# A fourth seven-product pair of gate/value tiles in the middle blocks of a fused attention and GEGLU kernel

## The chip, the cores and the metric

The kernel runs on one core of one Trainium2 chip. A core has TensorE (matmuls, written PE in the profile, with PEld for its weight loads), VectorE (DVE), ScalarE (ACT), GpSimd (POOL) and SyncE (SP, which here only issues DMAs). Each engine works through its own queue of instructions in order, and the queues are tied together by semaphores. The metric is device time in microseconds (us), as a median of several runs; one more execution was profiled.

## The reference

There are eight batches (B = 8) of eight heads, 576 rows and 64 columns per head. For each head, q is put through a softmax over its 64 columns and k through a softmax over its 576 rows; the head's output is softmax(q) @ (softmax(k)^T @ v). The heads stand side by side as x, with 4608 rows and 512 columns. Then comes a gated feed-forward layer:

```
g   = x @ w_gate          # 512 x 1536
val = x @ w_val           # 512 x 1536
out = (gelu(g) * val) @ w_out      # 1536 x 512, gelu in the erf form
```

Inputs and output are float32. The kernel works in float16 with float32 accumulation.

## The kernel before

**Blocks.** Rows are worked in blocks. Each batch gives a block of 512 rows (blocks 0 to 7), and the 64 rows left over of each batch are gathered in `xtr` and make block 8. The order is 0 to 6, then 8, then 7 (`order`). A block has two stages. The first makes `ht` = gelu(x w_gate) * (x w_val), transposed, in twelve tiles of 128 hidden columns (`NFI` = 12, `NO` = 6). The second multiplies `ht` by w_out.

**Plain tiles.** A plain tile needs four 512-column matmuls with w_gate ("6g" in a list of steps) and four with w_val ("6v"); `half` issues one such half. ScalarE applies gelu to the gate half, and VectorE multiplies both into `ht` (`scalar_tensor_tensor`, L624).

**Pairs.** Two tiles k and k + 3 can be made together with Strassen's seven products instead of eight (`pair_step`, `product_gv` at L605). Each product is four 256-column matmuls, so that a pair takes 28 of them, and it needs sums of blocks of the weights (`ws`, made by `sum_wgv`, L586) and of x (`xs`, made by `sum_x` on GpSimd, L592). A pair has four steps, k.1 to k.4:

- k.1: product 1 into bank pa, which ScalarE copies to pb (L660), and product 5 into pc, which is copied scaled to SBUF as `snq` ("snap", L640 on ScalarE, L638 on VectorE)
- k.2: product 6 added to pa, then snapped, and product 3 added to pc; VectorE adds pc and the snap into `cc` (L644)
- k.3: product 7 added to pa, VectorE adds pa and the first snap into `cc`; product 2 added to pb. pb gives the left half of tile k (`final`: gelu of 256 columns on ScalarE, L630, then a multiply on VectorE, L631). `upper` then does gelu on `cc` (L648) and GpSimd multiplies (L650), which gives the right halves of both tiles
- k.4: product 4 added to pa, which gives the left half of tile k + 3

All eight PSUM banks form one ring from block 2 on (`big`, `let_go`); a pair holds three of them until its results are read.

**The order within a block.** It is written out by hand. `THREE` is the list of steps of blocks 2 to 6: tiles 6 to 11 but for those in pairs 0, 1 and 2 are plain (pair 0 is tiles 0 and 3, and so on), and they alternate with the steps of the three pairs. `SIX`, for blocks 8 and 7, makes all twelve tiles in six pairs, two at a time. Letters in these lists are hooks: `ride(b, PR, letter)` issues what `at(b, PR, letter, ...)` has put there. In blocks 2 to 6, "a" and "n" are the two halves of the softmax of the next batch's q (`norm_pair`: a reduce at L240 and a reciprocal at L242 on VectorE, then two multiplies on GpSimd, L249), "t" is the DMA that transposes it (`unit_td`), "l" loads for the batch after that, and "s0", "u0", "s1", "u1" are sums of `ht` for the output (`sum_h`, L575; sums 1 and 2 on VectorE, 3 and 4 on GpSimd).

**The output.** `out_strassen` also uses seven products, of twelve matmuls each (`product`, L712), with sums of `ht` (`sh`, `s4`) and of w_out (`tw`, made by `sum_w`, L556). Hooks `ride(b, NS, i)` stand between products: at 0 the products of k and v for the next batch (`unit_kv4`), at 2 the casts of v and sums of weights, at 4 the next x (`unit_x4`), whose VectorE share is the casts at L192, and its sums. "e" holds the exps of q and k. The left-over rows of batch 0 have a norm and a transpose of their own (`norm_rem0`, `unit_trem`).

**The weight sums before.** Those for pairs 0 to 2 are spread over blocks 0 and 1 in full width (three tiles, 128 x 768). Those for pairs 6 to 8, which blocks 8 and 7 use, are made one or two per block in blocks 2 to 6. Sum 3 overwrites a quarter of the weights in place (`a21`), so the plain tile that needs it must be done.

Of the kernel before, what the change touches and what calls it, by code (L numbers as in the profile page):

```python
# [18 lines left out]
def kernel(  # L19
# [10 lines left out]
    nc = tc.nc  # L30

    B, H, S, D = q.shape
# [202 lines left out]
    def norm_pair(b, g, n0, engs):  # L235

        n = NC - n0
        e = buf(eq_b, b)[:, n0:NC, 2 * g * P:(2 * g + 2) * P].rearrange("p n (h d) -> p n h d", d=D)
        rq = att.tile([P, n, 4], f32, name="rq2", tag="rq2", bufs=2)
        nc.vector.reduce_sum(rq, e, axis=mybir.AxisListType.X)  # L240
        rrq = att.tile([P, n, 4], f32, name="rrq2", tag="rrq2", bufs=2)
        nc.vector.reciprocal(out=rrq, in_=rq)  # L242
        for j, eng in enumerate(engs):
            st[(b, "norm", 2 * g + j)] = (e[:, :, 2 * j:2 * j + 2], rrq[:, :, 2 * j:2 * j + 2], n)
            norm_mul(b, 2 * g + j, eng)

    def norm_mul(b, hp, eng="dve"):
# [328 lines left out]

    def sum_wgv(nm, i, k=0, n=NO // 2, eng="dve"):
        w = wg_sb if nm == "g" else wv_sb  # L580
        lo, hi = slice(k * P, (k + n) * P), slice((k + NO // 2) * P, (k + NO // 2 + n) * P)
        a11, a21, a12, a22 = w[:, 0:2, lo], w[:, 0:2, hi], w[:, 2:4, lo], w[:, 2:4, hi]
        t = [ws[(nm, k // NO)][:, j, :, k % NO * P:(k % NO + n) * P] for j in range(3)]
        o, a, b, op = {1: (t[0], a21, a22, ALU.add), 2: (t[1], t[0], a11, ALU.subtract),
                       3: (a21, a11, a21, ALU.subtract), 4: (t[2], a12, t[1], ALU.subtract)}[i]
        (nc.gpsimd if eng == "pool" else nc.vector).tensor_tensor(out=o, in0=a, in1=b, op=op)  # L586

    def sum_x(xt, xs=xs):
        b11, b12, b21, b22 = (xt[:, c:c + 2, r:r + 256] for c in (0, 2) for r in (0, 256))
# [4 lines left out]
    def product_gv(i, ps, xt, k, first):  # L594
# [3 lines left out]
        for t, w, nm in ((0, wv_sb, "v"), (1, wg_sb, "g")):  # L598
            ss = ws[(nm, k // NO)]
            for c in range(2):  # L600
# [6 lines left out]

    THREE = ("a 6g l 6v 0.1 9g 0.2 9v 0.3 7g 0.4 n 1.1 t 7v 1.2 10g 1.3 s0 10v 1.4 2.1 u0 8g 2.2 s1"  # L610
             " 8v 2.3 u1 11g 2.4 11v")
    SIX = ("0.1 6.1 0.2 6.2 0.3 6.3 0.4 1.1 6.4 7.1 s0 1.2 7.2 1.3 u0 7.3 1.4 2.1 7.4 8.1 s1 2.2"
           " 8.2 2.3 u1 8.3 2.4")
    steps = {b: (SIX if b >= B - 1 else THREE).split() for b in range(2, B + 1)}
    live = {}

    def half(b, xt, c, nm):
# [9 lines left out]
    def pair_step(b, xt, k, i):  # L627
        def final(ps, fi):
            gl = ffn.tile([P, 256], f32, name="glq", tag="gl")
            nc.scalar.activation(out=gl, in_=ps[:, 1], func=ACTF.Gelu)  # L630
            nc.vector.scalar_tensor_tensor(out=ht[:, fi, 0:256], in0=ps[:, 0], scalar=_H_SCALE,  # L631
                                           in1=gl, op0=ALU.mult, op1=ALU.mult)
            let_go(ps)

        def snap(ps, dve=False):
            sn = ffn.tile([P, 2, 256], f32, name="snq", tag="snq")
            if dve:
                nc.vector.tensor_scalar(out=sn, in0=ps, scalar1=_H_SCALE, scalar2=None, op0=ALU.mult)  # L638
            else:
                nc.scalar.activation(out=sn, in_=ps, func=ACTF.Copy, scale=_H_SCALE)  # L640
            return sn

        def add(o, ps, sn):
            nc.vector.scalar_tensor_tensor(out=o, in0=ps, scalar=_H_SCALE, in1=sn,  # L644
                                           op0=ALU.mult, op1=ALU.add)

        def upper(cc):
            nc.scalar.activation(out=cc[:, :, 1], in_=cc[:, :, 1], func=ACTF.Gelu,  # L648
                                 scale=1.0 / _H_SCALE)
            (nc.vector if k == NFI - NO // 2 - 1 else nc.gpsimd).tensor_tensor(  # L650
                out=ht[:, k:k + NO // 2 + 1:NO // 2, 256:512], in0=cc[:, :, 0], in1=cc[:, :, 1],
                op=ALU.mult)

        if i == 1:
            live["odd"] = odd = b > 2 and not live.get("odd", True)
            cc = cc_b if odd else ffn.tile([P, 2, 2, 256], f32, name="cc", tag="cc", bufs=1)
            pa = big([P, 2, 256], f32, "pga", True)
            product_gv(1, pa, xt, k, True)
            pb = big([P, 2, 256], f32, "pgb", True, True)
            nc.scalar.copy(out=pb, in_=pa)  # L660
            pc = big([P, 2, 256], f32, "pgc", True)
            product_gv(5, pc, xt, k, True)
            live[k] = [cc, pa, pb, pc, snap(pc, b >= B - 1)]
            return
        cc, pa, pb, pc, s5 = live[k]
        if i == 2:
            product_gv(6, pa, xt, k, False)
            s2 = snap(pa)
            product_gv(3, pc, xt, k, False)
            add(cc[:, 0], pc, s2)  # L670
            let_go(pc)
        elif i == 3:
            product_gv(7, pa, xt, k, False)
            add(cc[:, 1], pa, s5)
            product_gv(2, pb, xt, k, False)
            final(pb, k)
            if k == NFI - NO // 2 - 1:
                live["upper"] = lambda: upper(cc)
            else:
                upper(cc)  # L680
        else:
            product_gv(4, pa, xt, k, False)
            final(pa, k + NO // 2)
# [18 lines left out]
    def product(i, ps, first, ts=(0, 1), js=range(NO)):  # L702
        for j in js:
            for t in ts:
                c0, c1 = slice(t * P, (t + 1) * P), slice(256 + t * P, 256 + (t + 1) * P)
                a = {1: ht[:, j, c0], 2: ht[:, NO + j, c0], 3: s4[:, j, c0], 4: ht[:, NO + j, c1],
                     5: sh[1][:, j, c0], 6: sh[2][:, j, c0], 7: ht[:, j, c1]}[i]
                w = {1: wo_sb[:, j, 0:256], 2: wo_sb[:, NO + j, 0:256],
                     3: wo_sb[:, NO + j, 256:512]}.get(i)
                if w is None:  # L710
                    w = tw[{4: 4, 5: 1, 6: 2, 7: 3}[i]][:, j]
                nc.tensor.matmul(ps[t], a, w, start=(first and j == js[0] and (  # L712
                    t == ts[0] or ps[t].tensor is not ps[ts[0]].tensor)),
                                 stop=(j == js[-1]), skip_group_check=True)
# [7 lines left out]
    def out_strassen(b, last):  # L722
# [30 lines left out]

        js = (0, 1, 2, 3, 4, 5) if b < 2 else (0, 3, 1, 4, 2, 5)
        get("a")
        product(1, ps["a"], True, js=js[:4])
        ride(b, NS, 0)
        if b >= B - 1:
            pair_step(b, get_x(b), NFI - NO // 2 - 1, 4)
# [15 lines left out]
        product(6, ps["a"], False, js=js)  # L775
        s2 = snap("a")
        ride(b, NS, 2)
        cut = NO - 1 if b < B - 2 else NO
        product(3, ps["c"], False, js=js[:cut])
        if cut < NO:  # L780
            product(7, ps["a"], False, js=js)
# [125 lines left out]
    def load_2nd():  # L907
# [6 lines left out]
    at(0, NS, 5, L(unit_t, 1, 0))  # L914
    at(0, NS, 16, L(unit_kv, 1, 0), L(cast_v, 1, 4, 8), L(load_batch, 2, ((v, "v"),)),
       L(norm, 1, 3))
    at(0, NS, 17, L(unit_x, 1, 0, "act", True), L(unit_x, 1, 1, "act", True), L(sum_w, 1, "pool"),
       L(sum_w, 3, "pool"))
    at(0, NS, 7, L(exp, "q", 2))
    first1 = [[L(unit_t, 1, 1), L(unit_kv, 1, 1)],  # L920
              [L(unit_x, 1, 2, "dve"), L(preload, ACTF.Gelu)],
# [8 lines left out]

    at(1, FI, 2, L(unit_trem, 1))
    at(1, FI, 3, L(norm, 2, 2, "pool"), L(load_batch, 3, ((q, "q"), (k, "k"))))
    at(1, FI, 4, L(exp, "k", 2, 0, 4), L(norm, 2, 3, "pool"), L(sum_w, 2), L(sum_w, 4), make_s)
    at(1, FI, 5, L(cast_v, 2, 0, H))
    at(1, FI, 8, L(unit_td, 2))
    at(1, FI, 11, L(exp, "k", 2, 4, 8), L(exp, "q", 3))
# [3 lines left out]
    load_2 = lambda n: load_batch(n, ((v, "v"), (q, "q"), (k, "k")))  # L940
    for i, x in enumerate(("g1", "v1", "g2", "v2", "g4", "v4")):
        at(0, FI, 5 + i, L(sum_wgv, x[0], int(x[1])))
    at(1, FI, NFI - 1, L(sum_wgv, "g", 3, 0, NO // 2, "pool"), L(sum_wgv, "v", 3, 0, NO // 2, "pool"))
    for b in range(2, B):
        n = b + 1
        if n < B:
            at(b, PR, "a", L(norm_pair, n, 0, 0, ("pool", "pool")))
            at(b, PR, "n", L(norm_pair, n, 1, 0, ("pool", "pool")))
            at(b, PR, "t", L(unit_td, n))
        if n + 1 < B:  # L950
            at(b, PR, "l", L(load_2, n + 1))
            at(b, NS, 2, L(cast_v, n + 1, 0, H))
            at(b, PR, "e", L(exp, "q", n + 1), L(exp, "k", n + 1))
    at(4, PR, "l", load_rem0)
    at(4, PR, "e", exp_rem0)
    at(6, PR, "t", L(unit_trem, 0))
    for b in range(2, B - 1):
        n = b + 1
        at(b, NS, 4, L(unit_x4, n, ("act", "dve"), 0 if n == B - 1 else None))
        at(b, NS, 0, L(unit_kv4, n, True))  # L960
        if b < 6:
            at(b, NS, 4, L(preload, ACTF.Gelu))
        at(b, NS, 4, L(lambda n: sum_x(get_x(n)), n if n < B - 1 else B))
        if b == 5:
            at(b, NS, 4, norm_rem0)
    at(B, NS, 2, L(lambda: sum_x(get_x(B - 1), xs_b[1])))
    for b in range(2, B + 1):
        for j in range(NO // 2 - 1):
            at(b, PR, f"s{j}", L(sum_h, j, NO, (1,)), L(sum_h, j, NO, (3,), "pool"))
            at(b, PR, f"u{j}", L(sum_h, j, NO, (2,)), L(sum_h, j, NO, (4,), "pool"))  # L970
    for b, x in ((2, "g1"), (2, "g2"), (3, "v1"), (3, "v2"), (4, "g4"), (5, "v4"), (6, "g3"), (6, "v3")):
        at(b, NS, 2, L(sum_wgv, x[0], int(x[1]), NO, NO // 2))


    def ride(b, kind, i):
# [65 lines left out]
```

The softmax here doesn't subtract the row's maximum and nothing guards it: scores larger than these inputs give would overflow.

## Time and profile before

| | us |
|---|---|
| median of three runs | 297.39 (297.23 to 297.41) |
| profiled run | 297.5 |
| span of the profile, first to last instruction | 295.7 |
| busy: TensorE / VectorE / GpSimd / ScalarE | 285.9 / 221.0 / 200.5 / 182.0 |
| block 2, from its first plain half to the next block's | 30.93 |
| blocks 3, 4, 5, 6 | 30.43, 30.43, 30.42, 30.65 |

The busy times are sums over the whole span, so they say which engine is full and not where one waits. The span is shorter than the run's time because start and end of the program lie outside it; times in the text count from the span's start. Matmul records overlap (a 256-column matmul is recorded with 0.27 us but the next starts 0.11 us later), so costs on TensorE are read from one start to the next.

### The profile page before, as it was taken

To read this page: it belongs to the slowest core of one execution; us is meant where nothing else is said; L and a number is where in the kernel's file an instruction comes from. 1 tells how busy PE (TensorE), PEld (TensorE's weight loads), DVE (VectorE), ACT (ScalarE), POOL (GpSimd) and SP (SyncE) were. 2 spreads that over 40 slices of the span, in tenths; PEclk is the share of its full clock that TensorE was granted. 3 is DMA by queue.
4 is the path that set the end of the run, shared out by engine and by line. 5 is a ranking of instruction groups with operands and counts; after the bars stand their busy time and mean duration, and the time that the engine had idled before them with its cause. 6 is when DMAs were issued, how large, how long until landed. Compare 5 with 4: busy or idle time off the path is not lost. (4 is left out here: it accounts for less than half of the span.)

```text
span 295.7 us, 6184 instructions
## 1 busy us (share of the span) xinstructions
PE 285.9 (97%) x2401; PEld 198.4 (67%) x2401; DVE 221.0 (75%) x409; ACT 182.0 (62%) x295; POOL 200.5 (68%) x181
## 2 busy tenths in 40 slices
PE   3999999999999999999999999999999999999994
PEld 1544445445866696668666866677667888888884
DVE  2855878899778676867777676777677788958892
ACT  3763367776676668667756966695662477327640
POOL 1568647894386877687768776967886366673770
PEclk9999999999999999999999999999999999999999
DMA  6999999998069804970399029901140110023003
GB/s 216 373 382 390 400 391 392 339 321 228 3 205 383 124 3 153 375 183 3 136 344 249 2 96 337 279 2 73 71 88 13 72 73 2 1 64 80 2 0 144
DMA packets 54621, 51.72 MB, mean 175 GB/s; under 512 B 18496, under 2 KB 50496, under 8 KB 54592
## 3 DMA queue, kind: packets, MB, share of 16 engines
q1 hardware_dynamic: 52864, 49.49, 53.1%
q10 hardware_dynamic: 1728, 1.84, 1.9%
q8 instruction: 19, 0.31, 0.4%
q14 instruction: 10, 0.08, 0.1%
HBM read 37.75 MB, written 9.44 MB: 160 GB/s over the span
## 5 line engine op out<-in xcount | busy, mean ns | idle before, releaser
L466 PE MATMUL psg<-xt,wg_sb 128*128 128x512 f16 x216 | 57.8, 379 | 0.2 <-DVE xt L192 0.2
L466 PE MATMUL psv<-xt,wv_sb 128*128 128x512 f16 x216 | 57.4, 379 | 0.0
L249 POOL TENSOR_TENSOR eq<-eq,rrq 128x640 f16<-128x640 f16 (+1 forms) x27 | 34.8, 1307 | 20.2 <-DVE rrq L242 16.4
L712 PEld LDWEIGHTS <-ht 128*128 128x128 f16 x384 | 36.5, 98 | 8.8 <-issue 2.5
L466 PEld LDWEIGHTS <-wv_sb 128*128 128x128 f16 x216 | 21.0, 98 | 20.5 <-issue 1.0
L466 PEld LDWEIGHTS <-wg_sb 128*128 128x128 f16 x216 | 21.1, 98 | 18.6 <-issue 0.2
L575 POOL TENSOR_TENSOR s<-ht,sh 128x512 f16<-128x512 f16 x21 | 25.3, 1207 | 9.5 <-DVE sh L575 9.5
L575 POOL TENSOR_TENSOR ht<-ht 128x512 f16<-128x512 f16 x21 | 25.2, 1199 | 5.5 <-DVE sh L575 5.5
L605 PEld LDWEIGHTS <-wv_sb 128*128 128x128 f16 x216 | 20.9, 98 | 11.3 <-issue 1.8
L188 POOL CAST v<-vt 128x640 f16<-128x640 f32 x26 | 20.8, 841 | 8.6 <-PE pskv L342 7.1
L650 POOL TENSOR_TENSOR ht<-eq 128x512 f16<-128x512 f32 x12 | 15.4, 1286 | 16.0 <-ACT eq L648 15.8
L471 ACT ACTIVATE gl<-psg 128x512 f32<-128x512 f32 x24 | 13.8, 598 | 16.9 <-PE psg L466 14.7
L630 ACT ACTIVATE glq<-pgb 128x256 f32<-128x256 f32 x27 | 10.3, 380 | 21.9 <-PE pgb L605 14.0
L712 PE MATMUL psa<-tw,ht 128*128 128x256 f16 x192 | 23.4, 273 | 0.0
L605 PEld LDWEIGHTS <-wg_sb 128*128 128x128 f16 x216 | 21.1, 98 | 2.5
L212 ACT ACTIVATE ek<-kt 128x1280 f16<-128x1280 f32 (+1 forms) x11 | 19.1, 1748 | 5.6 <-DMA kt<-in_k_dram 3.6
L660 ACT COPY pgb<-pga 128x512 f32<-128x512 f32 x27 | 15.8, 584 | 9.8 <-PE pga L605 9.5
L622 ACT ACTIVATE gl<-psg 128x512 f32<-128x512 f32 x30 | 17.7, 590 | 5.7 <-PE psg L466 5.7
L472 DVE SCALAR_TENSOR_TENSOR ht<-psv,gl 128x512 f16<-128x512 f32 x24 | 16.0, 683 | 6.6 <-PE psv L466 6.5
L240 DVE TENSOR_REDUCE rq<-eq 128x20 f32<-128x1280 f16 (+1 forms) x12 | 17.1, 1428 | 4.7 <-ACT eq L212 4.7
L712 PEld LDWEIGHTS <-sh 128*128 128x128 f16 x192 | 18.8, 98 | 2.4 <-issue 0.3
L212 ACT ACTIVATE eq<-qt 128x2560 f16<-128x2560 f32 (+2 forms) x10 | 18.4, 1863 | 2.7 <-DMA qt<-in_q_dram 2.6
(164 smaller groups left out, 686.0 us busy)
## 6 DMA issues: line engine op xcount, KB each, us to landing
out_dram<-yo SPq DMA_DIRECT2D x15, 512.0 KB, 3.5
kt<-in_k_dram SPq DMA_DIRECT2D x7, 640.0 KB, 9.0
vt<-in_v_dram SPq DMA_DIRECT2D x7, 640.0 KB, 5.8
qt<-in_q_dram SPq DMA_DIRECT2D x7, 640.0 KB, 7.5
qt<-in_q_dram SPq DMA_DIRECT2D x8, 512.0 KB, 8.1
wost<-in_moe_w_out_dram SPq DMA_DIRECT2D x6, 512.0 KB, 7.9
kt<-in_k_dram SPq DMA_DIRECT2D x6, 512.0 KB, 9.4
vt<-in_v_dram SPq DMA_DIRECT2D x6, 512.0 KB, 6.3
```

Source lines behind the costliest of these rows:

```text
L188: nc.gpsimd.tensor_copy(out=dst, in_=src)
L212: nc.scalar.activation(out=dst[:, n0:NC, h0 * D:h1 * D].rearrange(o, d=D, **({"t": 2} if b >= QUAD else {})), in_=heads(tiles[(nm, b)], b, ...
L240: nc.vector.reduce_sum(rq, e, axis=mybir.AxisListType.X)
L249: (nc.gpsimd if eng == "pool" else nc.vector).tensor_tensor(out=e, in0=e, in1=rrq.unsqueeze(-1).to_broadcast((P, n, 2, D)), op=ALU.mult)
L466: nc.tensor.matmul(ps, w[:, ci, fi * P:(fi + 1) * P], xt[:, ci, :], start=(ci == 0), stop=(ci == HP - 1))
L472: nc.vector.scalar_tensor_tensor(out=ht[:, fi, :], in0=psv, scalar=_H_SCALE, in1=gl, op0=ALU.mult, op1=ALU.mult)
L575: (nc.gpsimd if eng == "pool" else nc.vector).tensor_tensor(out=o, in0=a, in1=b, op=op)
L605: nc.tensor.matmul(ps[:, t], a, x, start=(first and t == 0 and c == 0), stop=(c == 1), skip_group_check=True)
L622: nc.scalar.activation(out=live[c], in_=t, func=ACTF.Gelu)
L650: (nc.vector if k == NFI - NO // 2 - 1 else nc.gpsimd).tensor_tensor(out=ht[:, k:k + NO // 2 + 1:NO // 2, 256:512], in0=cc[:, :, 0], in1=c ...
L660: nc.scalar.copy(out=pb, in_=pa)
L712: nc.tensor.matmul(ps[t], a, w, start=(first and j == js[0] and (t == ts[0] or ps[t].tensor is not ps[ts[0]].tensor)), stop=(j == js[-1]), ...
```

## The change

The diff does five things.

1. Blocks 3 to 6 get a new list, `FOUR`: tiles 6 and 9 become pair 6, whose steps 1 to 4 take turns with those of pair 0. The plain tiles 7, 10, 8 and 11 stay, in a new order. "n" stands before the first product; its two GpSimd multiplies get a hook of their own, "m", after step 6.3. Pair 6's first snap is made on VectorE. Block 2 keeps three pairs.
2. Step 2.4 leaves the list in these blocks and is issued inside the output's product 1, after its first three tiles.
3. In these blocks the fourth sum of `ht` at "u1" goes from GpSimd to VectorE.
4. The weight sums for pair 6 alone (one tile wide, 128 x 256) are made in block 2: g1, v1, g2 and v2 at a new hook "w" ahead of step 0.1, and g4, v4, g3 and v3 in its output. The sums for pairs 7 and 8 are two tiles wide and follow in blocks 3 to 6. Sums g3 and v3 of the first set go from GpSimd in block 1 to VectorE in block 1's output. Of the sums of w_out, the first goes from GpSimd at the end of block 0 to VectorE in block 0, and the second from VectorE to GpSimd.
5. `norm_rem0` goes from the end of block 5 into block 6, hook "r", with its transpose behind it on SP's queue, past "t". In block 1's output product 7 comes after the whole of product 3.

```diff
-    THREE = ("a 6g l 6v 0.1 9g 0.2 9v 0.3 7g 0.4 n 1.1 t 7v 1.2 10g 1.3 s0 10v 1.4 2.1 u0 8g 2.2 s1"
+    THREE = ("a 6g l 6v w 0.1 9g 0.2 9v 0.3 7g 0.4 n m 1.1 t 7v 1.2 10g 1.3 s0 10v 1.4 2.1 u0 8g 2.2 s1"
              " 8v 2.3 u1 11g 2.4 11v")
+    FOUR = ("a 7g l 7v n 0.1 6.1 0.2 6.2 0.3 6.3 m 10g 0.4 6.4 1.1 t 10v 1.2 s0 8g u0 1.3 8v 1.4 r 2.1"
+            " 11g s1 2.2 11v 2.3 u1")
...
-    steps = {b: (SIX if b >= B - 1 else THREE).split() for b in range(2, B + 1)}
+    steps = {b: (SIX if b >= B - 1 else THREE if b == 2 else FOUR).split() for b in range(2, B + 1)}
...
-            live[k] = [cc, pa, pb, pc, snap(pc, b >= B - 1)]
+            live[k] = [cc, pa, pb, pc, snap(pc, b >= B - 1 or k >= NO)]
...
-        product(1, ps["a"], True, js=js[:4])
+        four = 2 < b < B - 1
+        cut = 3 if four else 4
+        product(1, ps["a"], True, js=js[:cut])
+        if four:
+            pair_step(b, get_x(b), NO // 2 - 1, 4)
+            product(1, ps["a"], False, js=js[cut:4])
...
-        cut = NO - 1 if b < B - 2 else NO
+        cut = NO - 1 if 1 < b < B - 2 else NO
...
-    at(0, NS, 17, L(unit_x, 1, 0, "act", True), L(unit_x, 1, 1, "act", True), L(sum_w, 1, "pool"),
-       L(sum_w, 3, "pool"))
+    at(0, NS, 17, L(unit_x, 1, 0, "act", True), L(unit_x, 1, 1, "act", True), L(sum_w, 3, "pool"),
+       L(sum_w, 2, "pool"))
...
-    at(1, FI, 4, L(exp, "k", 2, 0, 4), L(norm, 2, 3, "pool"), L(sum_w, 2), L(sum_w, 4), make_s)
+    at(1, FI, 4, L(exp, "k", 2, 0, 4), L(norm, 2, 3, "pool"), L(sum_w, 4), make_s)
...
-    at(1, FI, NFI - 1, L(sum_wgv, "g", 3, 0, NO // 2, "pool"), L(sum_wgv, "v", 3, 0, NO // 2, "pool"))
+    at(0, FI, NFI - 2, L(sum_w, 1))
+    at(1, NS, 2, L(sum_wgv, "g", 3), L(sum_wgv, "v", 3))
...
-            at(b, PR, "n", L(norm_pair, n, 1, 0, ("pool", "pool")))
+            at(b, PR, "n", L(norm_pair, n, 1, 0, ()))
+            at(b, PR, "m", L(norm_mul, n, 2, "pool"), L(norm_mul, n, 3, "pool"))
...
-    at(6, PR, "t", L(unit_trem, 0))
+    at(6, PR, "r", norm_rem0, L(unit_trem, 0))
...
-        if b == 5:
-            at(b, NS, 4, norm_rem0)
...
-            at(b, PR, f"u{j}", L(sum_h, j, NO, (2,)), L(sum_h, j, NO, (4,), "pool"))
-    for b, x in ((2, "g1"), (2, "g2"), (3, "v1"), (3, "v2"), (4, "g4"), (5, "v4"), (6, "g3"), (6, "v3")):
-        at(b, NS, 2, L(sum_wgv, x[0], int(x[1]), NO, NO // 2))
+            at(b, PR, f"u{j}", L(sum_h, j, NO, (2,)),
+               L(sum_h, j, NO, (4,), "dve" if j and 2 < b < B - 1 else "pool"))
+    for kind, i, xs_ in ((PR, "w", ("g1", "v1", "g2", "v2")), (NS, 2, ("g4", "v4", "g3", "v3"))):
+        for x in xs_:
+            at(2, kind, i, L(sum_wgv, x[0], int(x[1]), NO, 1))
+    for b, x in ((3, "g1"), (3, "g2"), (4, "v1"), (4, "v2"), (5, "g4"), (5, "v4"), (6, "g3"), (6, "v3")):
+        at(b, NS, 2, L(sum_wgv, x[0], int(x[1]), NO + 1, 2))
```

More of the change, by code (lines that the diff above doesn't have):

```diff
@@ L242, in norm_pair @@
         nc.vector.reciprocal(out=rrq, in_=rq)
+        for j in range(2):
+            st[(b, "norm", 2 * g + j)] = (e[:, :, 2 * j:2 * j + 2], rrq[:, :, 2 * j:2 * j + 2], n)
         for j, eng in enumerate(engs):
-            st[(b, "norm", 2 * g + j)] = (e[:, :, 2 * j:2 * j + 2], rrq[:, :, 2 * j:2 * j + 2], n)
             norm_mul(b, 2 * g + j, eng)
@@ L575, in sum_h, with sum_wgv @@
             (nc.gpsimd if eng == "pool" else nc.vector).tensor_tensor(out=o, in0=a, in1=b, op=op)
-    def sum_wgv(nm, i, k=0, n=NO // 2, eng="dve"):
+    def sum_wgv(nm, i, k=0, n=NO // 2):
         w = wg_sb if nm == "g" else wv_sb
@@ L585, in sum_wgv @@
                        3: (a21, a11, a21, ALU.subtract), 4: (t[2], a12, t[1], ALU.subtract)}[i]
-        (nc.gpsimd if eng == "pool" else nc.vector).tensor_tensor(out=o, in0=a, in1=b, op=op)
+        nc.vector.tensor_tensor(out=o, in0=a, in1=b, op=op)
     def sum_x(xt, xs=xs):
```

## The prediction, written before the changed kernel was run

> **What bounds the kernel now.** I read the page first (busy shares), then what TensorE waits for, then busy time by stretch, then the timelines of TensorE, VectorE and GpSimd around block starts.
>
> ```profile
> PE 285.9 (97%) x2401; PEld 198.4 (67%) x2401; DVE 221.0 (75%) x409; ACT 182.0 (62%) x295; POOL 200.5 (68%) x181
> ...
> PEclk9999999999999999999999999999999999999999
> ```
>
> TensorE is busy 97% of a 295.7 us span at full clock, so any matmul time removed is removed from the span, and any wait put into TensorE's queue is added. A busy PE is not a PE at its peak, so I take cost from start-to-start times (start, length, line):
>
> ```profile
> 178.44 1.03 PE L466 MATMUL psv<-xt,wv_sb 128*128 128x512 f16 x4
> 179.30 0.38 PE L605 MATMUL pga<-xs,wv_sb 128*128 128x256 f16 x2
> 179.52 0.38 PE L605 MATMUL pga<-xs,wg_sb 128*128 128x256 f16 x2
> ```
>
> A plain half tile (four 512-column matmuls) takes 179.30 - 178.44 = 0.866 us; two 256-column ones take 0.2185 us. Blocks 3, 4 and 5 take 30.43, 30.43 and 30.42 us: the same program at the same pace. Parts add to about 30.13 (12 x 0.866 + 42 x 0.2185 + 84 x 0.1093 for the output + 0.75 for kv + 0.64 for x), so little slack is there to win.
>
> TensorE's few waits are where a VectorE result comes late:
>
> ```profile
> 73.80 0.39 PE L712 MATMUL psb<-wo_sb,ht 128*128 128x256 f16 x2 [0.25 <-DVE ht L472]
> ```
>
> Its neighbours start at 72.30 with ten matmuls (1.09), so it is really 0.41 late.
>
> **What the Trainium skill says.** *TensorE: Matmul & The Clock Gate*, "Back-to-back issue gap", prices an isolated warm gap at N/2.4 + 2.5 ns: 215.8 and 109.2 ns for 512 and 256 columns; the trace has 216.4 and 109.3. The table at the head of that page calls VectorE's and GpSimd's queues strict FIFO; the trace agrees (an instruction waits behind older ones even if ready). *SBUF — State Buffer*, "Who interferes with whom": a VectorE instruction with two SBUF inputs and a GpSimd one that reads SBUF take one port as an exclusive lock for a whole instruction. The trace agrees closely:
>
> ```profile
> 60.80 2.89 DVE L556 TENSOR_TENSOR tw<-wo_sb,tw 128x1536 f16<-128x1536 f16 x2
> 60.92 1.96 POOL L249 TENSOR_TENSOR eq<-eq,rrq 128x640 f16<-128x640 f16 x1 [0.40 <-DVE rrq L232]
> 67.33 1.26 DVE L575 TENSOR_TENSOR ht<-ht 128x512 f16<-128x512 f16 x1
> 66.49 1.80 POOL L586 TENSOR_TENSOR wg_sb<-wg_sb 128x768 f16<-128x768 f16 x1
> ```
>
> The L249 multiply (usually 1.25) lasts until 62.88, and the second of the VectorE pair ends 0.81 later; L575 (0.42 alone) issued at 67.33 ends at 68.59, 0.30 after GpSimd's 68.29. The two engines alternate, one instruction each.
>
> **1. Matmuls.** A plain pair of tiles costs 4 x 0.866 = 3.46 us; the seven-product pair 14 x 0.2185 = 3.06. Saved 0.40 a block, four blocks (3 to 6): **-1.6 us**. Nothing hides TensorE, so this is all on the path.
>
> **2. The start of blocks 3 to 6.** VectorE's queue there in block 5, which starts on TensorE at 174.08:
>
> ```profile
> 174.62 1.47 DVE L240 TENSOR_REDUCE rq<-eq 128x20 f32<-128x1280 f16 x1
> 176.13 0.28 DVE L242 RECIPROCAL rrq<-rq 128x20 f32<-128x20 f32 x1
> 176.32 0.63 DVE L624 SCALAR_TENSOR_TENSOR ht<-psv,gl 128x512 f16<-128x512 f32 x1
> 178.88 0.69 DVE L644 SCALAR_TENSOR_TENSOR eq<-pgc,snq 128x512 f32<-128x512 f32 x1 [1.93 <-ACT snq L640]
> ```
>
> Times from the start of a block: the gate of the plain tile issues at 2.24 and holds VectorE 0.54. The new order puts "n" (reduce and reciprocal, 1.71 issue to issue, as at 174.62) straight behind it: 2.78 to 4.49. Only then comes the new snap of pair 6 (a 128x512 copy out of PSUM, 0.63 to 0.69 by L744 and L638): done at about 5.15. TensorE: two half tiles end at 1.75, then products 1 and 5 of pair 0, 1 and 5 of pair 6, 6 and 3 of pair 0, 6 of pair 6, seven times 0.437: at 4.81 it wants product 3 of pair 6, which overwrites the bank that the snap reads. Hand-over from VectorE to TensorE is about 0.06. Wait: 5.21 - 4.81 = 0.4 a block. Bounds: 0.2 (shorter overlap) to 0.6; never below 0. Everything on TensorE queues behind it. **+1.6 us**.
>
> **3. Later in those blocks.** Added a block: ScalarE a copy, a snap, a gelu of 0.6 each and smaller finals, less two plain gelus (+1.4); VectorE about +1.5 and a 0.42 sum taken from GpSimd; GpSimd +1.27 for L650, -1.16 for that sum. I followed the queues on. The pair adds finish before product 4 of pairs 0 and 6 (7.2 and 8.2 against 8.2 and 8.7); GpSimd's "m" multiplies end near 12.9, as in before, so the transposing DMA starts at the same place in the block and SP's queue behind it (two stores, six loads) does not move; the exps that need it start about 22. Three places have under 0.1 to spare: product 4 of pair 1 behind sh1, sh2 and an add; product 4 of pair 2, which now sits after six output matmuls (0.66) in place of a half tile (0.87); and tile 5 in product 1, which needs 2.4's final: 0.25 + 0.38 + 0.42 + hand-overs = 1.15 against 1.19 of matmuls. The wait before 2.4 is 0.11 to 0.17 a block now and comes out at about 0.06: **-0.2** (bounds -0.5 to 0.4); the other two **+0.1** (0 to 1.2).
>
> **4. "w" in block 2.** Four sums of 128x256 f16 go behind the first gate. Alone each would hold VectorE 0.2 (from 0.42 and 0.55 for 512 and 768 elements) and fit into idle time. But GpSimd is then in one run of work:
>
> ```profile
> 84.62 1.15 POOL L592 TENSOR_TENSOR xs<-xt 128x512 f16<-128x512 f16 x1
> 85.73 1.15 POOL L592 TENSOR_TENSOR xs<-xt,xs 128x512 f16<-128x512 f16 x1
> 86.84 2.48 POOL L249 TENSOR_TENSOR eq<-eq,rrq 128x640 f16<-128x640 f16 x2
> 84.98 0.63 DVE L624 SCALAR_TENSOR_TENSOR ht<-psv,gl 128x512 f16<-128x512 f32 x1
> 87.54 0.69 DVE L644 SCALAR_TENSOR_TENSOR cc<-pgc,snq 128x512 f32<-128x512 f32 x1 [1.93 <-ACT snq L640]
> 88.77 0.68 DVE L644 SCALAR_TENSOR_TENSOR cc<-pga,snq 128x512 f32<-128x512 f32 x1
> 89.70 0.38 PE L605 MATMUL pga<-xs,wv_sb 128*128 128x256 f16 x2
> ```
>
> By turns: sum 1 behind xs at 85.73, done 85.95; sum 2 behind the last xs, 87.15; sums 3 and 4 behind one multiply each, 88.5 and 89.8. Then the add, the gate of 9v and the second add, 0.6 each: 91.65 in place of 89.45. Product 4 of pair 0, which accumulates into that bank, starts at 91.7 and not at 89.70: **+2.0 us** (bounds 0, if all four slip in between, and 2.7). What follows on VectorE moves as much as TensorE does.
>
> **5. End of block 2.** Four small sums replace two of 768, taking turns with four v casts (0.68 each): they end about 111.5, and the add at 111.17 moves 0.3. The xt casts behind it end just when the next block's fourth matmul needs them (cast end 113.85, matmul 113.87), so all of it shows: **+0.3** (0 to 0.7). In blocks 3 to 6 two sums of 512 fit before the add.
>
> **6. Blocks 0 and 1.** w_out's first sum moves to VectorE near 36.8, where GpSimd is idle and tile 11 of block 0 is not needed before 42: nothing. GpSimd loses the two L586 sums at 66.49 to 70.08 that hold up VectorE; the gates of tiles 10 and 11 come earlier and the wait at 73.80 goes: **-0.4** (-0.45 to 0). These sums go to VectorE at the end of block 1, among the casts: 78.5 to 80.3, with the adds then about as late as now: 0 (-0.3 to 0.4). norm_rem0 and its transpose, moved past the "t" transpose on SP, have over 6 us before x is wanted: 0.
>
> **Sum:** -1.6 + 1.6 - 0.2 + 0.1 + 2.0 + 0.3 - 0.4 = **+1.8 us**. The profiled run was 297.5 with a span of 295.7; the median of the three is 297.39, so I add the sum to that: **299.2**.
>
> **Rivals.** About 0.2% (0.6 us) is what a measurement here can tell from no change.
> - *Both queues wait* (steps 2 and 4): 299.2, own range 298.1 to 300.6, chance 0.60. For: locks and FIFO order show in before. Against: gaps of 0.2 decide.
> - *VectorE's idle time hides the new work*: neither step waits; -1.6 - 0.2 - 0.4 = -2.2, 295.2, chance 0.12. For: VectorE is idle 1.93 at both places. This ends on the other side; it decides if snap ends before 4.75 and the sums before 87.6.
> - *Only one waits*: step 2 alone gives -1.6 + 1.6 - 0.2 + 0.1 - 0.4 = -0.5, 296.9; step 4 alone -1.6 - 0.2 + 0.1 + 2.0 + 0.3 - 0.4 = +0.2, 297.6; chance 0.18. For: each rests on its own margin. Against: the same queue feeds both.
> - *The short margins of step 3 fail as well*: up to 0.3 in each of four blocks, 300.4 and up, chance 0.10.
>
> Range: 296.8 to 301.0 leaves out the full gain and the worst end. Faster 0.15, same 0.13, slower 0.72 (the single-wait cases split over the 0.6 us bounds).
>
> **What would show it.** Right: blocks 3 to 6 near 30.4, with a gap of 0.4 before product 3 of pair 6 behind the snap; block 2 longer by about 2, with VectorE's L587 sums lasting over 1 us each; no wait in psb in block 1. Wrong: sums of 0.3 each, a snap issued before 4.1, or blocks at 30.0.

## The result and the profile after

The changed kernel takes 301.73 us (median of four runs, 301.66 to 301.85); the kernel before takes 297.36 beside it. The ratio is 1.0148, 95% interval 1.013 to 1.0166: slower by 4.4 us, where +1.8 was forecast and 301.0 was the end of the range.

Page of the changed kernel, busy times:

```profile
PE 284.4 (95%) x2449; PEld 202.7 (68%) x2449; DVE 238.1 (79%) x435; ACT 187.7 (63%) x307; POOL 195.8 (65%) x179
...
PEclk9999999999999999999999999999999999999999
```

TensorE does 1.5 us less work at the same clock, and yet the span went from 295.7 to 300.0. So the loss is idle time on TensorE. The three largest of TensorE's waits behind the warm-up (total, times, longest):

```profile
PE psa L715 <- DVE ht L634: 2.4, 3, 0.8
PE pga L606 <- DVE cc L647: 2.0, 2, 1.7
PE pgc L606 <- DVE snq L641: 1.1, 4, 0.5
```

Each of the three lines is a VectorE result that comes late, and none of them was there before. The view counts from the recorded end of the matmul before; recorded matmuls overlap, so the waits below are taken against the time at which the matmul was due, and are 0.15 to 0.2 longer. The lengths of the blocks on TensorE, first plain half to the next block's, say where:

| | before | after | |
|---|---|---|---|
| start of block 2 | 82.29 | 81.97 | -0.32 |
| block 2 | 30.93 | 32.45 | +1.52 |
| block 3 | 30.43 | 31.26 | +0.83 |
| block 4 | 30.43 | 31.28 | +0.85 |
| block 5 | 30.42 | 31.57 | +1.15 |
| block 6 | 30.65 | 30.89 | +0.24 |

**Block 2, as forecast.** VectorE, GpSimd and TensorE in the timeline (start, length):

```profile
85.17 1.24 DVE L587 TENSOR_TENSOR kt<-wv_sb 128x256 f16<-128x256 f16 x1
86.34 1.35 DVE L587 TENSOR_TENSOR kt<-kt,wg_sb 128x256 f16<-128x256 f16 x1
87.61 1.35 DVE L587 TENSOR_TENSOR kt<-kt,wv_sb 128x256 f16<-128x256 f16 x1
...
90.07 0.67 DVE L647 SCALAR_TENSOR_TENSOR cc<-pga,snq 128x512 f32<-128x512 f32 x1
...
85.06 1.20 POOL L593 TENSOR_TENSOR xs<-xt,xs 128x512 f16<-128x512 f16 x1
86.23 2.58 POOL L250 TENSOR_TENSOR eq<-eq,rrq 128x640 f16<-128x640 f16 x2
...
88.04 1.03 PE L467 MATMUL psg<-xt,wg_sb 128*128 128x512 f16 x4
90.80 0.39 PE L606 MATMUL pga<-xs,wv_sb 128*128 128x256 f16 x2 [1.74 <-DVE cc L647]
```

With GpSimd idle, such a sum is recorded with 0.28 (at 111.98, at the end of the block). These three (sums 2 to 4, written to what the view calls `kt`) end at 86.41, 87.69 and 88.96: the first 0.15 after GpSimd's at 86.26, the others one GpSimd multiply later each. So the add before product 4 ends only at 90.74. The half tile at 88.04 is worth 0.87, so product 4 was due at 88.91 and is 1.89 late. The block grows by only 1.52, because a wait at its start is gone (see **Block 1**).

**Start of blocks 3 to 6, as forecast.** Block 5, VectorE first, then TensorE:

```profile
180.05 1.48 DVE L240 TENSOR_REDUCE rq<-eq 128x20 f32<-128x1280 f16 x1
...
181.76 0.63 DVE L641 TENSOR_SCALAR snq<-pgc 128x512 f32<-128x512 f32 x1
...
181.33 0.60 PE L606 MATMUL pga<-xs,kt 128*128 128x256 f16 x4
182.44 0.60 PE L606 MATMUL pgc<-xt,kt 128*128 128x256 f16 x4 [0.50 <-DVE snq L641]
```

The snap stands behind the reduce and ends at 182.39; product 3 of pair 6, due at 181.77, starts 0.67 late. In blocks 3, 4 and 6 it starts 0.36 late, which makes 1.75 in all. Block 5 has 0.67 in e6's trace below too, but 0.40 in e1's and 0.36 in e3's, with the same order of work at its start; why is open.

**End of the pairs in block 3, not forecast.** VectorE, GpSimd, TensorE:

```profile
134.52 0.42 DVE L576 TENSOR_TENSOR sh<-sh,ht 128x512 f16<-128x512 f16 x1
134.97 1.51 DVE L576 TENSOR_TENSOR s<-ht,sh 128x512 f16<-128x512 f16 x1
136.40 0.41 DVE L634 SCALAR_TENSOR_TENSOR ht<-pga,glq 128x256 f16<-128x256 f32 x1
...
134.93 1.27 POOL L653 TENSOR_TENSOR ht<-cc 128x512 f16<-128x512 f32 x1 [1.82 <-ACT cc L651]
...
135.68 0.39 PE L715 MATMUL psa<-wo_sb,ht 128*128 128x256 f16 x2
136.87 0.39 PE L715 MATMUL psa<-wo_sb,ht 128*128 128x256 f16 x2 [0.79 <-DVE ht L634]
```

The fourth sum of u1, moved to VectorE, issues 0.04 us after GpSimd's multiply of pair 2 and waits for all of it: 1.51 instead of 0.42. The multiply that writes tile 5 (L634) stands behind it, though its gelu on ScalarE had ended at 135.19, and product 1 of the output needs tile 5: it was due at 135.90 and starts at 136.87, 0.97 late. Blocks 4 and 5 show the same wait, at 168.14 and 199.71, with the same 0.04 between the two issues; the three waits make 2.90. Block 6 doesn't, because there the sum issues first, by 0.11 us, and GpSimd's multiply (1.45 in place of 1.27) is the one that waits:

```profile
229.31 0.43 DVE L576 TENSOR_TENSOR s<-ht,sh 128x512 f16<-128x512 f16 x1
...
229.42 1.45 POOL L653 TENSOR_TENSOR ht<-cc 128x512 f16<-128x512 f32 x1 [1.36 <-ACT cc L651]
```

Block 6 has, a little earlier, a wait of its own: `norm_rem0`'s multiply on GpSimd holds up a sum of `ht` on VectorE (225.57, 1.25 long), and product 4 of pair 2 starts 0.39 late, at 228.67.

**Block 1.** psb runs through, where before it stopped at 73.80:

```profile
72.12 1.47 PE L715 MATMUL psb<-wo_sb,ht 128*128 128x256 f16 x12
```

The casts of x at the end of this block come earlier too, at 81.28 for 82.07 before. So a wait at the start of block 2 is gone, which the prediction doesn't count. TensorE, before and after:

```profile
82.29 0.90 PE L466 MATMUL psg<-xt,wg_sb 128*128 128x512 f16 x3
83.41 0.38 PE L466 MATMUL psg<-xt,wg_sb 128*128 128x512 f16 x1 [0.22 <-DVE xt L192]
...
81.97 1.03 PE L467 MATMUL psg<-xt,wg_sb 128*128 128x512 f16 x4
```

Before, the fourth matmul was due at 82.94 and came 0.47 late; now the four run in one piece. Which of the edits in block 1 brought the casts forward wasn't tried.

### The profile page after: what moved, and what is told of

Its sections match the earlier page's. It is cut to its first block, busy times and chain, and to the rows that moved or that the text cites. A ratio compares the mean times of both kernels' runs of the same rounds, so it can differ in the third digit from the quotient of the medians.

```text
span 300.0 us, 6329 instructions
## 1 busy us (share of the span) xinstructions
PE 284.4 (95%) x2449; PEld 202.7 (68%) x2449; DVE 238.1 (79%) x435; ACT 187.7 (63%) x307; POOL 195.8 (65%) x179
## 5 line engine op out<-in xcount | busy, mean ns | idle before, releaser
L467 PE MATMUL psg<-xt,wg_sb 128*128 128x512 f16 x184 | 49.3, 379 | 0.0
L467 PE MATMUL psv<-xt,wv_sb 128*128 128x512 f16 x184 | 49.2, 379 | 0.0
L653 POOL TENSOR_TENSOR ht<-eq 128x512 f16<-128x512 f32 x14 | 17.8, 1273 | 17.9 <-ACT eq L651 17.9
L576 POOL TENSOR_TENSOR s<-ht,sh 128x512 f16<-128x512 f16 x17 | 20.7, 1220 | 10.2 <-DVE sh L576 10.2
L188 POOL CAST v<-vt 128x640 f16<-128x640 f32 x26 | 19.0, 771 | 12.8 <-PE pskv L343 11.3
L653 POOL TENSOR_TENSOR ht<-cc 128x512 f16<-128x512 f32 x15 | 19.4, 1294 | 10.1 <-ACT cc L651 10.1
L663 ACT COPY pgb<-pga 128x512 f32<-128x512 f32 x31 | 18.3, 589 | 9.7 <-PE pga L606 9.4
L472 ACT ACTIVATE gl<-psg 128x512 f32<-128x512 f32 x24 | 13.8, 597 | 16.6 <-PE psg L467 16.5
L643 ACT ACTIVATE snq<-pga 128x512 f32<-128x512 f32 x31 | 18.5, 597 | 6.8 <-PE pga L606 6.2
L606 PE MATMUL pga<-xs,wv_sb 128*128 128x256 f16 x100 | 19.1, 272 | 2.1 <-DVE cc L647 2.0
```

The source lines that it names most:

```text
L188: nc.gpsimd.tensor_copy(out=dst, in_=src)
L467: nc.tensor.matmul(ps, w[:, ci, fi * P:(fi + 1) * P], xt[:, ci, :], start=(ci == 0), stop=(ci == HP - 1))
L606: nc.tensor.matmul(ps[:, t], a, x, start=(first and t == 0 and c == 0), stop=(c == 1), skip_group_check=True)
```

## The experiments

**Theory.** Three waits in VectorE's queue, each its own: "w" behind the port in block 2, pair 6's snap behind "n", and u1's fourth sum behind the port ahead of tile 5. **Rivals**: VectorE is simply too full for the new work, so that a wait taken away in one place comes back in the next; or the fourth pair itself, with its interleaving, costs what it saves. The first three runs start from the changed kernel and take one part back each; the fourth takes back all three.

### Run e1_sum_pool: u1's fourth sum back on GpSimd

```diff
-               L(sum_h, j, NO, (4,), "dve" if j and 2 < b < B - 1 else "pool"))
+               L(sum_h, j, NO, (4,), "pool"))
```

> Undoes one part: the fourth sum of ht at u1 goes back from VectorE to GpSimd in blocks 3 to 6. Theory (port lock): on VectorE this sum issues 0.04 us after GpSimd's L653 has taken the shared port, lasts 1.51 instead of 0.42, and tile 5's final behind it makes product 1 wait 0.97 us in blocks 3, 4 and 5; without it those waits go and 2.5 to 3.5 us with them: about 298.5. Rival A (step 2.4 stands too late in the output whatever VectorE does): at least 0.5 us of the wait stays in each block, 300.5 or more. Rival B (VectorE is simply too full in blocks 3 to 6, a queue that anything lengthens): only the 0.42 us per block of the sum itself is won, about 300.

Measured: 298.79, ratio to before 1.0044 (1.0035 to 1.0053). TensorE at the same place, in block 3:

```profile
134.95 0.82 PE L343 MATMUL pskv<-v,ek 128*64 128x65 f16 x40
135.70 0.61 PE L715 MATMUL psa<-wo_sb,ht 128*128 128x256 f16 x4
```

Four matmuls in one run: the wait is gone. The gain is 2.94 us, for the 2.90 read from the trace; by blocks 3 to 6 it is 0.94, 0.93, 1.20 and -0.07. The wait of "w" stays as it was. That at the snap is 0.35 to 0.41 in all four blocks, so block 5 has 0.27 less of it, a part of the gain that isn't the sum's.

### Run e2_snap_act: pair 6's first snap on ScalarE

```diff
-            live[k] = [cc, pa, pb, pc, snap(pc, b >= B - 1 or k >= NO)]
+            live[k] = [cc, pa, pb, pc, snap(pc, b >= B - 1)]
```

> Undoes one part: the first snap of pair 6 is made on ScalarE, as for the other pairs, not on VectorE behind the reduce and reciprocal of n. Theory: the wait before product 3 of pair 6 (0.36 us, in block 5 0.66) goes in each of four blocks, 1.4 to 1.7 us: about 300.2; the waits at tile 5 stay at 0.97. Rival (the wait is for the bank and only changes its releaser, to ScalarE or to the adds that still stand behind the reduce): less than 0.5 us won, 301.3.

Measured: 300.56, 1.0098 (1.0066 to 1.013). The snap now runs on ScalarE at 118.40, while VectorE reduces. TensorE:

```profile
118.84 0.60 PE L606 MATMUL pga<-xs,kt 128*128 128x256 f16 x4
119.28 0.60 PE L606 MATMUL pgc<-xt,kt 128*128 128x256 f16 x4
```

Product 3 follows product 6 after 0.44, with no wait. The gain is 1.17, less than the 1.75 of the waits; by blocks 3 to 6 it is 0.29, 0.24, 0.52 and 0.21. Most of the rest comes back a little later in the same blocks: product 4 of pair 1, in time in the changed kernel, is now 0.07 to 0.15 late in each (e8 below shows why).

### Run e3_w_pool: the sums of "w" on GpSimd

Sums 1 of w_gate and w_val go behind "n", sums 2 to the output's hook 0, all four on GpSimd.

```diff
-    for kind, i, xs_ in ((PR, "w", ("g1", "v1", "g2", "v2")), (NS, 2, ("g4", "v4", "g3", "v3"))):
+    for kind, i, xs_, eng in ((PR, "n", ("g1", "v1"), "pool"), (NS, 0, ("g2", "v2"), "pool"),
+                              (NS, 2, ("g4", "v4", "g3", "v3"), "dve")):
...
```

> Moves one part: in block 2 the four weight sums of hook w go to GpSimd, two at hook n (where it waited 1.65 us for the second reduce) and two at the start of the output. Theory: product 4 of pair 0 in block 2 no longer starts 1.9 us late, about 299.8. Rival (the second add was late for another reason, for instance the casts of x at the block's start): the wait stays above 1 us, 300.8 or more.

Measured: 299.82, 1.009 (1.0058 to 1.0122). On GpSimd the first two sums take 0.67 us each, at 93.34 and 93.97. TensorE in block 2:

```profile
90.76 1.03 PE L467 MATMUL psg<-xt,wg_sb 128*128 128x512 f16 x4
91.62 0.38 PE L606 MATMUL pga<-xs,wv_sb 128*128 128x256 f16 x2
```

Product 4 follows the half tile after 0.86, with no wait. The gain is 1.91, against a wait of 1.89. Block 2 takes 30.75, 1.70 less: 0.2 comes back at its end, where product 7 now waits for an add.

### Run e4_three: all three

> All three edits of the first three kernels at once. Theory: the three waits are independent and their gains add up to 6 to 7 us, so 295.0 to 295.7: faster than the kernel before by about 0.6%, as only the saved matmuls (1.6 us) and a little from block 1 are left. Rival (a queue of work that is merely moved): the gains overlap, and it ends at 297 to 298.5, no better than before.

Measured: 296.12, 0.9952 (0.9936 to 0.9967). Blocks 2 to 6 take 30.74, 30.06, 30.10, 30.11 and 30.71. The three single gains add to 6.02; together they give 5.61, as block 5's 0.27 at the snap is in both e1's gain and e2's. Blocks 3 to 5 are 0.31 to 0.37 shorter than before, so the fourth pair pays there once its neighbours on VectorE are put elsewhere, and the second rival falls. Of the first, a small part stands: the waits that came back in e2 and e3 are there in e4 too, about 0.7 us against the 5.61 won.

### Run e5_before_sum: the moved sum in the kernel before

```diff
-            at(b, PR, f"u{j}", L(sum_h, j, NO, (2,)), L(sum_h, j, NO, (4,), "pool"))
+            at(b, PR, f"u{j}", L(sum_h, j, NO, (2,)),
+               L(sum_h, j, NO, (4,), "dve" if j and 2 < b < B - 1 else "pool"))
```

> The kernel before with one part of the change alone: the fourth sum of u1 (s4 of tiles 1, 2) on VectorE in blocks 3 to 6, in the list of before. Theory (the sum harms only because the last step of pair 2 stands behind it inside product 1): there tile 11's half tiles, 0.87 us each, and tile 5's products follow it before product 1 asks for tile 5, so its wait for the port is hidden; 297.4 (297.1 to 297.8). Rival (VectorE is the wrong engine for this sum wherever it stands, 0.8 to 1 us in three or four blocks): 299.8 to 301.

Measured: 297.37, 1.0 (0.9992 to 1.0009). The sum alone costs nothing. But that can have two reasons, and the run doesn't tell them apart. In block 3 the sum issues first, at 132.19 against 132.29 for GpSimd's multiply, and in all four blocks it takes 0.42, so it never waited for the port. And had it ended 1.1 us later, at 133.7, tile 5 would by my estimate still have been in time: its multiply, which takes 0.42, would have ended at about 134.1, and product 1 reaches tile 5 at 134.78.

### Run e6_sum_late: the same sum, same engine, behind tile 5

```diff
             product(1, ps["a"], False, js=js[cut:4])
+            sum_h(NO // 2 - 2, NO, (4,))
```

The sum leaves "u1" in blocks 3 to 6.

> The changed kernel with the fourth sum of u1 still on VectorE in blocks 3 to 6, but issued after the last step of pair 2, so that the multiply which writes tile 5 stands ahead of it in the queue. Theory (queue order behind a locked port is the cause, not the engine's load): the gain of the run with the sum on GpSimd, 298.8 (298.4 to 299.2), no wait before tile 5 in product 1. Rival (VectorE's load or the lock on the multiply itself): 300.5 or more, the wait stays.

Measured: 298.90, 1.0051 (1.0037 to 1.0064). VectorE, GpSimd and TensorE in block 3:

```profile
135.36 0.42 DVE L634 SCALAR_TENSOR_TENSOR ht<-pga,glq 128x256 f16<-128x256 f32 x1 [0.30 <-ACT glq L633]
135.71 0.91 DVE L576 TENSOR_TENSOR s<-ht,sh 128x512 f16<-128x512 f16 x1
...
135.06 1.27 POOL L653 TENSOR_TENSOR ht<-cc 128x512 f16<-128x512 f32 x1 [1.81 <-ACT cc L651]
...
135.81 0.61 PE L715 MATMUL psa<-wo_sb,ht 128*128 128x256 f16 x4
```

The sum still waits for GpSimd's multiply (0.91 instead of 0.42), but tile 5's multiply is ahead of it, and TensorE doesn't wait. That multiply, with one input in PSUM, runs beside GpSimd's in its usual 0.42, so it isn't itself held by the port. The gain is that of e1 within 0.1 us with the engine's work unchanged: the place in the queue was the cause.

### Run e7_24_list: step 2.4 back before the output

From e4: "2.4" at the end of `FOUR`, and product 1's first four tiles in one piece.

> The run with all three repairs, but the last step of pair 2 back before the output: it follows u1 at the end of the list, and product 1 runs its first four tiles in one piece. Theory: product 4 then has only product 2 (0.44 us) to hide product 7's add (0.25 + 0.68 + 0.06, about 1.0), so it waits 0.5 a block, and tile 5's final has 0.87 us of output matmuls to hide 1.15, another 0.3: 4 x 0.8 = 3.3 us more than with the three repairs, 299.4 (298.0 to 300.0). Rival (the place inside product 1 is worth nothing): 296.1 to 296.5.

Measured: 298.62, 1.004 (1.0025 to 1.0056): 2.5 us more than e4, 0.62 in each of blocks 3 to 6. TensorE in block 3:

```profile
131.48 0.38 PE L606 MATMUL pgb<-xt,wg_sb 128*128 128x256 f16 x2
132.37 0.38 PE L606 MATMUL pga<-xs,wv_sb 128*128 128x256 f16 x2 [0.51 <-DVE cc L647]
...
133.77 0.82 PE L343 MATMUL pskv<-v,ek 128*64 128x65 f16 x40
```

Product 4 waits 0.67 (due at 131.70) for the add. The second wait that I expected, 0.3 at tile 5, isn't there: the kv matmuls of 0.75 us stand between, which my expectation had left out. So the new place of 2.4 gains 0.62 a block.

### Run e8_rem0: the remainder's norm where it was

From e4: `norm_rem0` back to block 5's end and its transpose to "t".

> The run with all three repairs, and the remainder's norm and its transpose where the kernel before has them (end of block 5, and t of block 6). Theory: in block 6 the remainder's multiply on GpSimd holds the port and makes sh1 of tiles 1, 2 (1.25 in place of 0.42) and with it the add ahead of product 4 of pair 2 late, real wait 0.3 to 0.4; without it 295.8 (295.4 to 296.1). Rival (it falls elsewhere in VectorE's queue at the end of block 5, at the cost of the xt casts): 296.1 to 296.6.

Measured: 295.95, 0.995 (0.9937 to 0.9962), against e4's 0.9952. The wait in block 6 is gone and that block takes 30.45 in place of 30.71, but the time moves by less than the two intervals can tell. Another wait in these blocks is left. VectorE and TensorE in block 6:

```profile
215.60 0.72 DVE L576 TENSOR_TENSOR sh<-ht 128x512 f16<-128x512 f16 x1
...
216.29 1.03 PE L467 MATMUL psv<-xt,wv_sb 128*128 128x512 f16 x4
217.44 0.38 PE L606 MATMUL pga<-xs,wv_sb 128*128 128x256 f16 x2
```

Product 4 of pair 1, due at 217.16, is 0.28 late; in blocks 3, 4 and 5 it is late by 0.08, 0.13 and 0.13. The first sum of `ht`, which stands on VectorE ahead of the add that product 4 needs, takes 0.51 to 0.72 in place of 0.42: GpSimd's two multiplies of "m" end only at 216.04 here. This is read from the trace; no run moved "m".

### Runs e10_ends_pool and e11_b1_sums: two small waits behind adds

Both from e8, whose TensorE still waits 0.2 us twice for an add into `yo`, in blocks 1 and 2. e10 puts the last four small sums of block 2 on GpSimd, e11 the third sums of block 1:

```diff
-                               (NS, 2, ("g4", "v4", "g3", "v3"), "dve")):
+                               (NS, 1, ("g4", "v4", "g3", "v3"), "pool")):
```

```diff
-    at(1, NS, 2, L(sum_wgv, "g", 3), L(sum_wgv, "v", 3))
+    at(1, FI, NFI - 1, L(sum_wgv, "g", 3, 0, NO // 2, "pool"), L(sum_wgv, "v", 3, 0, NO // 2, "pool"))
```

> The run with the three repairs and the remainder's norm put back, and in block 2 the last four small sums (g4, v4, g3, v3) on GpSimd behind its sums for the output, ahead of the v casts, in place of VectorE among those casts. Theory (step 5 of the prediction: on VectorE these four delay the add, so product 7 and the next block's start wait 0.2 to 0.3): 0.2 to 0.3 us less than the 295.95 of that run, 295.7. Rival (four sums of 0.6 us on GpSimd delay the casts and with them the sums of x, or the order there never mattered): 295.9 to 296.5.

> The run with the three repairs and the remainder's norm put back, and in block 1 the two third sums of weights (g3, v3 of 768 elements) on GpSimd at the last tiles, as in the kernel before. Theory (step 6 of the prediction: there they hold the port against VectorE's sums and gates, psb waits 0.4 us; on VectorE at the end of the block they cost 0.2 at an add): 0.2 us more than 295.95, 296.15, with the psb wait back. Rival (no difference): 295.95.

Measured: e10 295.71 (0.9947, 0.9933 to 0.996), block 2 down from 30.74 to 30.46. e11 295.60 (0.9942, 0.9929 to 0.9954), block 1 down from 33.33 to 33.14: the opposite of what I expected. Both intervals overlap that of e8, so it is the blocks that show these gains and not the times. In e11 the add's wait goes, and the wait in psb doesn't come back. VectorE and GpSimd in e11:

```profile
60.84 0.93 DVE L557 TENSOR_TENSOR tw<-wo_sb,tw 128x1536 f16<-128x1536 f16 x1
...
65.51 1.80 POOL L587 TENSOR_TENSOR wg_sb<-wg_sb 128x768 f16<-128x768 f16 x1
```

The pair of sums starts 0.98 earlier than before (66.49), and VectorE has one w_out sum here where before it had two (2.89 us). GpSimd's four casts of v between that sum and the pair took 3.71 before and take 2.70 here. So it seems that psb came in time because that w_out sum left VectorE's queue, where it held up both engines, and not because g3 and v3 left GpSimd's. The w_out sum wasn't tried by itself.

### Run e12_all: e10 and e11 together

> Both last edits together, on top of the three repairs and the remainder's norm put back: the last four small sums of block 2 on GpSimd, and the third sums of block 1 on GpSimd at the last tiles. Theory (each takes its own 0.2 us wait at an add away, in different blocks): the gains add, 295.95 - 0.24 - 0.35 = 295.4, no wait behind an add into yo. Rival (they disturb each other through GpSimd's queue, or each gain is only scatter): 295.6 to 296.0.

Measured: 295.34, 0.9927 (0.9914 to 0.9941). Blocks 1 and 2 take 33.15 and 30.46, so both gains are there, and it is the fastest of all, 2.2 us below its 297.49 of before. Behind the warm-up, TensorE's list of waits holds a single one of 0.3; those at product 4 of pair 1, 0.08 to 0.27, are still there but too short for the list.

## Why the prediction fell short

Sign and mechanism were right: work moved onto VectorE stood behind the shared port or behind a long reduce, and TensorE paid. The size failed, by 2.6 us, and one term, of 2.8, accounts for it; the errors of the others nearly cancel.

- **Step 3, the term that failed.** "The other two +0.1 (0 to 1.2)" came out at 2.9, all of it at tile 5. I had tile 5's chain at 1.15 against 1.19 us of matmuls, with 0.42 for the sum. That is its length if it gets the port. GpSimd's multiply and this sum both issue at the end of pair 2's third step, within about 0.1 us of each other, and a step that loses the port there pays what is left of the other instruction, 1.1 us. So the place had two outcomes, about 0 or about 1.0 in each block, and three of four blocks fell on the second. The fourth rival named the place, but priced it at "up to 0.3" a block: as a margin that fails by a little, not as a lock that is lost. With 1.0 in three or four blocks it would have read 302 to 303. *SBUF — State Buffer*, "Who interferes with whom", in the Trainium skill, says that issue order decides who blocks and that the loser blocks fully; 134.93 against 134.97 and 1.51 against 0.42 show it. I had used this rule for "w" and not for the sum.
- **Step 1** (-1.6) **and the rest of step 3** (-0.2): the changed kernel's blocks 3 to 6 are 3.07 longer than before. Without their waits at tile 5 (2.90), at the snap (1.75) and in block 6 (0.39) that leaves -2.0. In e8, where those waits are out, the same blocks are only 1.26 shorter than before. Of the rest, 0.6 is the wait at product 4 of pair 1, the first of step 3's three short places: it was in time in the changed kernel, and fails by a little once the snap no longer delays TensorE ahead of it.
- **Step 2** (+1.6): 1.75 in the trace, of which e2 wins 1.2, as the wait at product 4 of pair 1 takes its place in part.
- **Step 4** (+2.0): 1.9, with the taking of turns as written, instruction by instruction.
- **Step 5** (+0.3): less than 0.1 in the changed kernel, where product 7 starts 0.63 after the last matmuls of x began, for 0.55 before. It shows only once "w" is out of the way: 0.24 to 0.28 by e10.
- **Step 6** (-0.4): block 1 is 0.15 shorter, as the psb wait of 0.41 is gone and a new one of 0.2 behind an add has come, and the wait of 0.47 at the start of block 2 is gone as well, which makes -0.6. The other 0.17 of block 2's earlier start lies ahead of block 1, whose start differs by up to 0.5 between the traces. The reason given for psb, GpSimd's two L586 sums, doesn't stand by itself: with them back (e11) the psb wait stays away. And `norm_rem0`, put at 0, costs 0.39 in block 6.

"VectorE's idle time hides it" (295.2) was wrong for this version. That e12 ends near it, at 295.34, doesn't bear it out: much of the new work had to be put on GpSimd and ScalarE first, and the wait at product 4 of pair 1 is still there.

## What to carry to other kernels

When an instruction with two SBUF inputs is put on VectorE, list what GpSimd may issue within some tenths of a microsecond of it, and price the place twice, as won and as lost; here a lost port cost most of the other instruction (1.1 us of 1.27), and a chain with 0.04 us to spare is then not a small risk but one of 1 us in each block. It isn't a matter of chance either: in the traces of the changed kernel, e2 and e3, the same three blocks lose the port by 0.04 and block 6 wins it by about 0.1. Put such an instruction behind the one that TensorE waits for, or on the engine where nobody waits for it. And when a large change loses, take back its parts one at a time before giving it up: here three small moves, none of which touched a matmul, turned +1.5% into -0.5%.

## What the runs showed of the hardware

- One instruction has two lengths, by 0.15 us of issue order: u1's sum takes 1.51 us in blocks 3 to 5 (issued 0.04 after GpSimd's multiply) and 0.43 in block 6 (issued 0.11 ahead).
- In e3's profiled execution, which took 302.44 us where its median is 299.82, a norm multiply of block 1 lost the port to a w_out sum by 0.07 us. VectorE and GpSimd:

```profile
48.66 3.72 DVE L250 TENSOR_TENSOR eq<-eq,rrq 128x640 f16<-128x640 f16 x1
...
48.59 3.10 POOL L557 TENSOR_TENSOR tw<-wo_sb 128x1536 f16<-128x1536 f16 x1
```

In the changed kernel's own profile this multiply issues at 48.29, before GpSimd's sum at 48.82, and takes 1.24. The transposes behind it on TensorE wait 2.17 us, and block 1 takes 35.67 us where it takes 33.33 in the changed kernel's profile. Neither instruction was touched by e3's edit, so the same code can win or lose the port in different executions. The other five executions of e3, at 299.69 to 299.91, left no trace, so it isn't shown that they win it, but the 2.34 us of this block are nearly all that this one is longer by.
